# Products with w_o1 and w_o2 in pieces of three matmuls, placed behind the block products; sums of squares for w_g, w_v and w_o2

## The chip, the core and the metric

The kernel runs on one core of a Trainium2 chip. The metric is device time in microseconds (us) of one execution, the median of several.

## What is computed

Softmax attention over channels, then two feed-forward layers on the 6016 tokens. `q` and `k` are normalised over the tokens, a 256x256 softmax is made of them, and `v` is multiplied by it.

```python
def _attn_ref(q, k, v, tau):
    qn = q / (np.linalg.norm(q, axis=1, keepdims=True) + 1e-06)
    kn = k / (np.linalg.norm(k, axis=1, keepdims=True) + 1e-06)
    s = kn.transpose(0, 2, 1) @ qn / tau
    ...
    return (v @ a).astype(np.float32)          # a: softmax of s, 256 x 256

def _moe_ref(x, w_in, w_out):                  # 256 -> 2048 -> 256
    h = x @ w_in
    g = h * (1.0 / (1.0 + np.exp(-1.702 * h)))
    return (g @ w_out).astype(np.float32)

def _moe2_ref(x, w_gate, w_val, w_out):        # 256 -> 1536 -> 256
    gate = 1.0 / (1.0 + np.exp(-(x @ w_gate)))
    val = x @ w_val
    return (gate * val @ w_out).astype(np.float32)
```

In the kernel `w_in` and `w_o1` are the weights of the first layer, `w_g`, `w_v` and `w_o2` those of the second. The weights come as 64-bit floats and are turned into 32-bit floats on the chip.

## The kernel before

Every large product is made of float16 matmuls in threes: both operands are split into a high and a low half, and high by high, high by low and low by high are summed in PSUM (`prod3`). The halves need a common power of two per operand, which is why each weight, each block of `v` and each block of the first layer's output is first reduced to a bound of its size (`w_top`, `w_max`, `v_max`, `y_max`), scaled, and split (a high half by ACT, a low half by DVE).

The tokens are cut into 12 blocks (11 of 512, one of 384). The program has three stretches. First `q` and `k` are read, their product summed over the tokens and the 256x256 softmax made; it is folded into `w_in`, which gives `m_t`. Then the first layer runs block by block. A block has 8 steps; a step makes two rows of 128 hidden channels (`h_unit`), which from block 1 on takes 7 products of 3 matmuls of 256 columns instead of 8 (`seven`, a Strassen-like scheme in which ACT copies a partial sum out of PSUM three times and DVE adds one twice, so that products of one step wait on ACT and DVE; block 0 uses `eight`, plain products of 512 columns). ACT applies the gelu, ACT or DVE rounds to the high half `gh`, DVE makes the low half `gl`. Two steps later `y_unit` multiplies by `w_o1`: 12 matmuls of 512 columns, summed over the block in two PSUM banks, `("acc", 0)` and `("acc", 1)`. Last, the second layer runs the same way: `gv_unit` with 7 products a step and 12 steps a block, and `o_unit`, 6 matmuls of 512 columns with `w_o2` into the same two banks, one step later. During blocks 1 to 6 of the first layer the weights of the second layer are also read, converted (`w_f32`), reduced (`w_top`), scaled and split (`w_split`, `s_piece`), all on DVE and ACT.

The order on every engine is set by a planner (class `Plan`). Operations are written down with what they read and write and with an estimate of their cost. The planner picks the operation that can start first by those estimates; of those on the same engine that could start within `EPS` (0.1 us) of it, it takes the one with the lowest rank. The rank is the place at which the operation was written, plus `plan.delay` at that moment. Each engine then executes its operations strictly in that order on the chip, whatever the real durations are.

Four PSUM banks, `("rot", 0)` to `("rot", 3)`, serve the products of two steps in turn (`ax_pair`); a product of step u+2 waits until ACT has read the pair of step u. Three buffers hold `gh` and `gl` (`NG` = 3), so the high half of step u+3 waits until the product with step u is done; nine further steps of blocks 0 and 1 have buffers of their own. Banks `("acc", 0)` and `("acc", 1)` serve at the start also for the scale of `w_o1` and of the second block of `v` (`p2_ops`, L282 in the trace).

Of the kernel before, what the change touches and what calls it, by code (L numbers as in the profile page):

```python
# [17 lines left out]
PW = 512  # L18
# [8 lines left out]
W_AT, W_STEP = ((1, 4), (2, 4), (3, 2)), 2  # L27
S_AT = (73, 75, 86, 97)
BY_POOL = ("in", "o1")
LOOSE = ("o1",)  # L30

V0_DELAY, V1_DELAY, O1_DELAY, O1_SPLIT, SUM_FIRST = -60, 150, 80, -20, 60


POOL_PEN, GH_DVE = -0.3, 0.3
EPS, HOLD, DMA_WAIT = 0.1, 0.2, 1.2

REBIAS = 2.0**-112
# [123 lines left out]
def fused_kernel(ctx, tc, q, k, vt, tau, w_in, w_o1, w_g, w_v, w_o2, outt):  # L162
# [15 lines left out]
    C, NT = vt.shape  # L178
    CC = C // P
# [31 lines left out]
    T = {}  # L211
# [867 lines left out]
    def pair(u):  # L1079
        f0 = u // 2 * (NB // P) + u % 2  # L1080
        return f0, f0 + 2
# [101 lines left out]
    def y_unit(b, u):  # L1183
        n = blocks[b][1]
        name = f"1_{b}_{u}"
        for z, f in enumerate(pair(u)):
            def mul(e, z=z, f=f):
                for c in range(CC):
                    cs = slice(f * C + c * P, f * C + (c + 1) * P)
                    g = T[name]  # L1190
                    prod3(bank(ACC_BANK[c]), n, wo1_h[:, cs], wo1_l[:, cs], g[0][:, z, :n], g[1][:, z, :n],
                          u == 0 and z == 0, u == NU - 1 and z == 1)

            i = f * C // PW
            r = [g_keys[b, u], ("glo", name), ("wh", "o1", i), ("wl", "o1", i)]
            o = op(mul, ("pe", 0.002532 * n), r=r, w=ACC_BANK)
            if b < 2:
                slot_users.append(o)
        if u == NU - 1:
            def evac(e, c):  # L1200
                nc.scalar.copy(out=y_blk(b)[:, c * n : (c + 1) * n], in_=bank(ACC_BANK[c])[:, :n])

            for c in range(CC):
                op(lambda e, c=c: evac(e, c), ("act", 0.07 + 0.00095 * n), r=[ACC_BANK[c]],
                   w=[("yf", b, c)], after=w_users.get("g", []) + w_users.get("v", []) if b >= YX + 2 else ())
# [49 lines left out]
    for (b, f0), (nm, src) in zip(W_AT, (("o2", w_o2), ("g", w_g), ("v", w_v))):  # L1255
        np_w = src.shape[1] * src.shape[2] // PW
        pos = b * NF1 + f0
        at(*divmod(pos, NF1), w_start(nm, src))
        for i in range(np_w):

            at(*divmod(pos if i < NRAW // 2 else pos + 3 + W_STEP * (i - NRAW // 2), NF1), w_load, nm, i)
            if nm not in LOOSE or not w_src[nm][1]:
                at(*divmod(pos + 2 + W_STEP * i, NF1), w_top, nm, i)
            at(*divmod(pos + 2 + W_STEP * i, NF1), w_f32, nm, i)
        pos += 4 + W_STEP * np_w
        at(*divmod(pos, NF1), w_max, nm)
        pos += 5
        at(*divmod(pos, NF1), lambda nm=nm, after=(): w_scale(nm, after, TOP if nm == "o2" else TOP2))
        if nm == "o2":
            for i in range(np_w):  # L1270
                at(*divmod(pos + 1 + i, NF1), w_split, nm, *[lambda x=x: late_pools()["o2"][x] for x in range(2)], i)
        if nm == "v":
            for x, pos in enumerate(S_AT):
                at(*divmod(pos, NF1), *((s_ratio,) if x == 0 else (s_piece, x - 1)))
# [119 lines left out]
    def o_unit(b, j):  # L1394
        t0, n = blocks[b]
        name = f"2_{b}_{j}"
        keys = ACC_BANK

        def mul(e):
            u = T[name]  # L1400
            for c in range(CC):
                cs = slice(j * C + c * P, j * C + (c + 1) * P)
                prod3(bank(keys[c]), n, *[w[:, cs] for w in late_pools()["o2"]], u[0][:, :n], u[1][:, :n],
                      j == 0, j == NF2 - 1)

        i = j * C // PW
        op(mul, ("pe", 0.002532 * n), r=[g_keys[2, b, j], ("glo", name), ("wh", "o2", i), ("wl", "o2", i)], w=keys)
        if j == NF2 - 1:
            kt = ring("vraw")

            def scale(e):
                T["osc", b] = vec(f"osc{b % 2}")
                nc.vector.tensor_mul(T["osc", b], qb[b], first["ko"])

            def evac(e, c):
                if c == 0:
                    T["ob", b] = v_p.tile([P, CC * NB], F32, tag="v_raw", name=f"ob{b}")
                nc.scalar.activation(
                    out=T["ob", b][:, c * n : (c + 1) * n], in_=bank(keys[c])[:, :n], func=AF.Copy, scale=T["osc", b]
                )  # L1420

            def store(e, c):
                nc.sync.dma_start(out=outt[c * P : (c + 1) * P, t0 : t0 + n], in_=T["ob", b][:, c * n : (c + 1) * n])

            op(scale, ("dve", 0.07), r=[("qb", b), ("k2",)], w=[("osc", b % 2)])
            for c in range(CC):
                kc = kt if c == 0 else ("ob", b, c)
                op(lambda e, c=c: evac(e, c), ("act", 0.07 + 0.00097 * n), r=[keys[c], ("osc", b % 2)] + ([kt] if c else []),
                   w=[kc])
                op(lambda e, c=c: store(e, c), ("dma", 1.0), r=[kc, kt], w=[("out", b, c)])  # L1430
# [60 lines left out]
```

## Time and profile before

| | us |
|---|---|
| median of three runs | 1084.67 |
| lowest and highest | 1082.95, 1086.24 |
| the profiled execution, its own time | 1085.58 |
| its span, first to last instruction | 1083.8 |
| PE busy (7236 matmuls) | 1051.2 |
| DVE busy | 811.4 |
| ACT busy | 724.4 |
| POOL busy | 46.2 |

The profile names an instruction by its line: L1003 are the products of `seven`, L979 to L981 the three matmuls of `prod3` (with `wo` the first layer's second product, with `wo_h` and `wo_l` the second layer's, with `vo,m_t` the plain products of block 0). L1012 are the copies of `seven` on ACT, L1017 its adds on DVE. Matmuls are pipelined: the next one starts before the last has ended, so the distance from start to start is what a matmul costs, and an idle time in brackets counts only from the modelled end of the one before.

### The profile page before, as it was taken

Reading aid. Unit: us, or ns where it says so; the run is one execution under the profiler, and the core shown is the slowest. Engines: PE = TensorE matmul, PEld = TensorE weight load, DVE = VectorE, ACT = ScalarE, POOL = GpSimd, SP = SyncE. Lnnn points to the kernel's source line nnn. Section 1 sums busy time; section 2 is a strip of 40 time slices with the busy share of each in tenths; the row PEclk is TensorE's granted clock in tenths of the full one; section 3 lists DMA queues with packets and bytes.
Section 4 is the critical chain, followed back from the end, with each engine's and each line's share of the span. In section 5 each row is a group of like instructions: output and inputs, shape, how many; then the busy total and the mean of one; then the engine's idle time right before and its main releaser. Section 6 shows DMA issues by size and latency. Waiting matters only on the chain.

```text
span 1083.8 us, 18237 instructions
## 1 busy us (share of the span) xinstructions
PE 1051.2 (97%) x7236; PEld 724.9 (67%) x7236; DVE 811.4 (75%) x1548; ACT 724.4 (67%) x1438; POOL 46.2 (4%) x54
## 2 busy tenths in 40 slices
PE   7988999999999999999999999999999999999998
PEld 6833566666655666666677777777777777777776
DVE  6999999998889677667586666667667667566655
ACT  6786576777757566555576666666767667667665
POOL 1441000000000000000000000000000000000000
PEclk9999999999999999999999999999999999999999
DMA  8940213320000000000000000000000000000000
GB/s 305 371 149 1 98 40 117 98 78 21 1 20 20 1 21 15 1 2 1 1 1 2 21 1 21 20 2 20 1 21 20 1 20 21 1 21 1 21 21 15
DMA packets 16165, 43.63 MB, mean 40 GB/s; under 512 B 1744, under 2 KB 3024, under 8 KB 16080
## 3 DMA queue, kind: packets, MB, share of 16 engines
q1 hardware_dynamic: 16080, 42.47, 11.3%
q8 instruction: 56, 0.92, 0.4%
q14 instruction: 29, 0.24, 0.1%
HBM read 36.31 MB, written 6.16 MB: 39 GB/s over the span
## 4 chain that ended last, share of the span: by engine, by line
PE 81%; DVE 10%; ACT 7%; issue 1%; DMA 1%; SPq 0%; ACTq 0%; DVEq 0%
PE ps L1003 42%; PE ps L980 12%; PE ps L981 11%; PE ps L979 11%; PE ps L717 4%; DVE gl L312 2%; ACT gf L1141 1%; DVE s_t L312 1%; DVE gf L1017 1%; DVE gh L1164 1%; ACT gf L1367 1%; DVE big L499 1%; DMA m_t<-in_q 1%; ACT gh L309 1%; DVE big L611 1%
## 5 line engine op out<-in xcount | busy, mean ns | idle before, releaser
L1003 PE MATMUL ps<-vo,s_t 128*128 128x256 f16 (+1 forms) x3024 | 354.2, 270 | 4.7 <-ACT ps L1012 1.9
L1003 PEld LDWEIGHTS <-s_t 128*128 128x128 f16 x3024 | 292.0, 98 | 73.0 <-issue 9.4
L1017 DVE TENSOR_TENSOR gf<-ps,m_t 128x256 f32<-128x256 f32 (+1 forms) x464 | 192.1, 415 | 151.3 <-PE ps L1003 85.5
L1012 ACT COPY m_t<-ps 128x256 f32<-128x256 f32 (+1 forms) x464 | 167.6, 367 | 149.7 <-PE ps L1003 149.3
L1003 PE MATMUL ps<-vo,m_t 128*128 128x256 f16 (+1 forms) x1848 | 231.7, 271 | 8.2 <-ACT m_t L1012 3.0
L1003 PEld LDWEIGHTS <-m_t 128*128 128x128 f16 x1848 | 179.3, 98 | 69.1 <-issue 12.7
L1385 DVE TENSOR_TENSOR gl<-gf,gh 128x512 f16<-128x512 f32 (+1 forms) x144 | 97.9, 680 | 58.1 <-ACT gh L1380 58.1
L980 PE MATMUL ps<-gl,wo 128*128 128x512 f16 (+1 forms) x348 | 130.2, 374 | 0.5 <-DVE gl L312 0.3
L979 PE MATMUL ps<-gh,wo 128*128 128x512 f16 (+1 forms) x348 | 130.2, 374 | 0.4 <-DVE p_v L285 0.4
L981 PE MATMUL ps<-gh,wo 128*128 128x512 f16 (+1 forms) x348 | 130.2, 374 | 0.0
L1380 ACT CAST gh<-gf 128x512 f16<-128x512 f32 (+1 forms) x135 | 82.3, 610 | 65.2 <-DVE gf L1373 65.0
L312 DVE SCALAR_TENSOR_TENSOR gl<-gf,sgi,gh 128x1024 f16<-128x1024 f32 (+1 forms) x87 | 109.0, 1256 | 3.3 <-ACT gh L309 2.0
L980 PE MATMUL ps<-gl,wo_h 128*128 128x512 f16 (+1 forms) x288 | 107.9, 375 | 0.5 <-DVE gl L1385 0.5
L1367 ACT ACTIVATE gf<-ps,sgb 128x512 f32<-128x512 f32 (+1 forms) x144 | 97.7, 678 | 16.0 <-PE ps L1003 12.5
L979 PE MATMUL ps<-gh,wo_h 128*128 128x512 f16 (+1 forms) x288 | 107.9, 375 | 0.5 <-ACT gh L1380 0.5
L981 PE MATMUL ps<-gh,wo_l 128*128 128x512 f16 (+1 forms) x288 | 107.9, 375 | 0.0
L1373 DVE SCALAR_TENSOR_TENSOR gf<-gf 128x512 f32<-128x512 f32 (+1 forms) x144 | 98.1, 681 | 12.5 <-ACT gf L1367 0.3
L1012 ACT COPY ps<-ps 128x256 f32<-128x256 f32 (+1 forms) x232 | 81.8, 358 | 24.8 <-PE ps L1003 22.4
L1141 ACT ACTIVATE gf<-ps,sgs 128x512 f32<-128x512 f32 (+1 forms) x88 | 59.4, 677 | 36.7 <-PE ps L1003 36.7
L1141 ACT ACTIVATE gf<-gf,sgs 128x512 f32<-128x512 f32 (+1 forms) x88 | 62.3, 711 | 19.2 <-DVE gf L1017 18.3
L981 PEld LDWEIGHTS <-wo 128*128 128x128 f16 x384 | 37.5, 98 | 45.8 <-issue 3.4
L1164 DVE TENSOR_SCALAR gh<-gf,sgi 128x1024 f16<-128x1024 f32 (+1 forms) x61 | 45.2, 743 | 23.2 <-ACT gf L1141 22.7
(217 smaller groups left out, 975.0 us busy)
## 6 DMA issues: line engine op xcount, KB each, us to landing
v_raw<-in_vt SPq DMA_DIRECT2D x11, 512.0 KB, 4.7
out_t<-ob SPq DMA_DIRECT2D x22, 256.0 KB, 2.0
m_t<-in_k SPq DMA_DIRECT2D x10, 512.0 KB, 5.9
m_t<-in_q SPq DMA_DIRECT2D x10, 512.0 KB, 6.8
s_t<-in_w_o SPq DMA_DIRECT2D x6, 512.0 KB, 3.8
s_t<-in_w_g SPq DMA_DIRECT2D x6, 512.0 KB, 3.8
s_t<-in_w_v SPq DMA_DIRECT2D x6, 512.0 KB, 3.9
big<-in_w_in SPq DMA_DIRECT2D x4, 512.0 KB, 6.4
```

The lines of the kernel that those rows point to most:

```text
L312: nc.vector.scalar_tensor_tensor(out=lo, in0=x, scalar=s, in1=h, op0=ALU.mult, op1=ALU.subtract)
L979: nc.tensor.matmul(ps[:, :n], w_h, x_h, start=first, stop=False)
L980: nc.tensor.matmul(ps[:, :n], w_h, x_l, start=False, stop=False)
L981: nc.tensor.matmul(ps[:, :n], w_l, x_h, start=False, stop=last)
L1003: nc.tensor.matmul(dst, l, r, start=start and y == 0, stop=y == 2, skip_group_check=True)
L1012: op(lambda e: nc.scalar.copy(out=dst, in_=bank(key)[:, :w]), ("act", 0.1 + w / 1150), r=[key], w=[wk], after=after)
L1017: nc.vector.tensor_add(val(half), bank(kw)[:, :w], other)
L1141: nc.scalar.activation(out=dst, in_=pair_ap(kx, w) if x == 0 else dst, func=AF.Gelu_apprx_sigmoid, scale=T[sk][0])
L1367: nc.scalar.activation(out=T[kf][:, :n].rearrange("p (x w) -> p x w", x=2), in_=pair_ap(kx, w), func=AF.Sigmoid, scale=T[sk])
L1373: nc.vector.scalar_tensor_tensor(out=v, in0=v, scalar=VSHIFT, in1=T[kf][:, :n], op0=ALU.mult, op1=ALU.mult)
L1380: nc.scalar.copy(out=T[name][0][:, :n], in_=T[kf][:, NB : NB + n])
L1385: nc.vector.tensor_sub(T[name][1][:, :n], T[kf][:, NB : NB + n], T[name][0][:, :n])
```

## The change

`y_unit` and `o_unit` hand each output half (c = 0 or 1) to the planner as an operation of its own, three matmuls that write one bank, where before one operation held both halves and wrote both banks. All of these pieces get 60 added to their rank (`FILL`, `FILL2`), so they stand behind products of `seven` that were written up to 60 operations later. And `w_g`, `w_v` and `w_o2` join `w_o1` in `LOOSE`: the bound on their size is taken from a sum of squares that ACT makes of the converted piece, where before DVE took the largest magnitude of the raw words.

```diff
-LOOSE = ("o1",)
+LOOSE = ("o1", "g", "v", "o2")
...
+FILL, FILL2 = 60, 60
...
     def y_unit(b, u):
...
+        plan.delay = FILL
         for z, f in enumerate(pair(u)):
-            def mul(e, z=z, f=f):
-                for c in range(CC):
+            for c in range(CC):
+                def mul(e, z=z, f=f, c=c):
                     cs = slice(f * C + c * P, f * C + (c + 1) * P)
                     g = T[name]
                     prod3(bank(ACC_BANK[c]), n, wo1_h[:, cs], wo1_l[:, cs], g[0][:, z, :n], g[1][:, z, :n],
                           u == 0 and z == 0, u == NU - 1 and z == 1)
 
-            i = f * C // PW
-            r = [g_keys[b, u], ("glo", name), ("wh", "o1", i), ("wl", "o1", i)]
-            o = op(mul, ("pe", 0.002532 * n), r=r, w=ACC_BANK)
...
+                o = op(mul, ("pe", 0.001266 * n), r=r, w=[ACC_BANK[c]])
...
+        plan.delay = 0
...
-            if nm not in LOOSE or not w_src[nm][1]:
+            if nm not in LOOSE or src.dtype != mybir.dt.int64:
                 at(*divmod(pos + 2 + W_STEP * i, NF1), w_top, nm, i)
...
+        plan.delay = FILL2
+        for c in range(CC):
+            def mul(e, c=c):
+                u = T[name]
                 cs = slice(j * C + c * P, j * C + (c + 1) * P)
                 prod3(bank(keys[c]), n, *[w[:, cs] for w in late_pools()["o2"]], u[0][:, :n], u[1][:, :n],
                       j == 0, j == NF2 - 1)
...
+            op(mul, ("pe", 0.001266 * n), r=[g_keys[2, b, j], ("glo", name), ("wh", "o2", i), ("wl", "o2", i)], w=[keys[c]])
+        plan.delay = 0
```

What the planner makes of it is seen in the order of the instructions. Lines of the changed kernel are one to three higher: its copies are L1013, its adds L1018, its `prod3` L980 to L982, its squares L466.

PE at the end of block 0, after the products of its sixth step (`vo` by `m_t`). Before, the scale of the second block of `v` (`eye_b`) and the products of the seventh step follow:

```order
L981 LDWEIGHTS m_t_85
L981 MATMUL ps_84<-vo_89,m_t_85 128x512
L282 LDWEIGHTS ones_b_249
L282 MATMUL ps_84<-eye_b_91,ones_b_249 128x128
L979 LDWEIGHTS m_t_85
L979 MATMUL ps_84<-vo_89,m_t_85 128x512
```

Now (`gh1_0_0` and `gl1_0_0` are the halves of block 0's first step, `wo1` is `w_o1`):

```order
L982 LDWEIGHTS m_t_85
L982 MATMUL ps_84<-vo_89,m_t_85 128x512
L980 LDWEIGHTS wo1_87
L980 MATMUL ps_84<-gh1_0_0_759,wo1_87 128x512
L981 LDWEIGHTS wo1_87
L981 MATMUL ps_84<-gl1_0_0_760,wo1_87 128x512
L982 LDWEIGHTS wo1_87
L982 MATMUL ps_84<-gh1_0_0_759,wo1_87 128x512
```

A second such piece follows, then the products of the seventh step, then four more pieces, and only then `eye_b`: pieces with c = 0 need only the other bank.

PE in block 3 of the second layer (`wo2` is `w_o2`, `gh2_3_2` the half of step 2). Before, all six matmuls of a step with `w_o2` stand in one run:

```order
L979 LDWEIGHTS wo2_h_882
L979 MATMUL ps_84<-gh2_3_2_7171,wo2_h_882 128x512
L980 LDWEIGHTS wo2_h_882
L980 MATMUL ps_84<-gl2_3_2_7172,wo2_h_882 128x512
L981 LDWEIGHTS wo2_l_883
L981 MATMUL ps_84<-gh2_3_2_7171,wo2_l_883 128x512
L979 LDWEIGHTS wo2_h_882
L979 MATMUL ps_84<-gh2_3_2_7171,wo2_h_882 128x512
L980 LDWEIGHTS wo2_h_882
L980 MATMUL ps_84<-gl2_3_2_7172,wo2_h_882 128x512
```

Now three of them stand between products of `seven` (11 products, 33 matmuls, come before the other three):

```order
L1004 LDWEIGHTS s_t_885
L1004 MATMUL ps_84<-vo_89,s_t_885 128x256
L980 LDWEIGHTS wo2_h_887
L980 MATMUL ps_84<-gh2_3_2_7179,wo2_h_887 128x512
L981 LDWEIGHTS wo2_h_887
L981 MATMUL ps_84<-gl2_3_2_7180,wo2_h_887 128x512
L982 LDWEIGHTS wo2_l_888
L982 MATMUL ps_84<-gh2_3_2_7179,wo2_l_888 128x512
L1004 LDWEIGHTS s_t_885
L1004 MATMUL ps_84<-vo_89,s_t_885 128x256
```

Over the whole program the matmuls of PE form 650 runs of one kind before and 1084 now.

ACT in block 1 of the first layer (L487 and L488 convert a piece of `w_o2`, L1141 and L1142 are gelus). Before:

```order
L1012 COPY ps_84<-ps_84 128x256
L487 ACTIVATE s_t_880<-s_t_880 128x512
L1012 COPY m_t_85<-ps_84 128x256 x2
L1141 ACTIVATE gf1_1_4_1312<-ps_84,sgs1_914 128x512
L1141 ACTIVATE gf1_1_5_1325<-ps_84,sgs1_914 128x512
```

Now:

```order
L1013 COPY m_t_85<-ps_84 128x256 x2
L488 ACTIVATE s_t_885<-s_t_885 128x512
L466 ACTIVATE junk_90,sums_o2_1236<-s_t_885 128x512
L1142 ACTIVATE gf1_1_4_1297<-ps_84,sgs1_970 128x512
L466 ACTIVATE junk_90,sums_o2_1236<-s_t_885 128x512
L1142 ACTIVATE gf1_1_4_1297<-gf1_1_4_1297,sgs1_970 128x512
```

The squares (L466, 18 more of them) stand in ACT's queue among gelus and copies; on DVE the 18 reductions of `w_o2`, `w_g` and `w_v` are gone.

## Rows read from the trace of the kernel before

**Rows 1.** Profile page, part 1: busy us (share of the span) and instructions by engine.

```profile
PE 1051.2 (97%) x7236; PEld 724.9 (67%) x7236; DVE 811.4 (75%) x1548; ACT 724.4 (67%) x1438; POOL 46.2 (4%) x54
```

**Rows 2.** Busy time by stretch: stretch, length, PE, PEld, DVE, ACT, POOL, clock, DMA.

```profile
93.00:105.00 12.00, 9.57 (x38) 3.90 (x36) 11.93 (x18) 8.38 (x10) 0.00 (x0) 0.86 0.01 1
...
145.00:185.00 40.00, 39.34 (x263) 25.52 (x261) 39.11 (x79) 28.19 (x55) 1.05 (x3) 1.00 0.27 93
185.00:225.00 40.00, 38.85 (x253) 24.54 (x252) 39.90 (x81) 30.23 (x56) 2.51 (x3) 1.00 0.34 106
...
303.00:346.00 43.00, 38.79 (x248) 24.83 (x246) 37.32 (x64) 26.96 (x53) 0.68 (x2) 0.96 0.00 1
346.00:555.00 209.00, 208.49 (x1450) 139.27 (x1449) 147.80 (x264) 123.88 (x249) 4.04 (x9) 1.00 0.03 8
```

**Rows 3.** PE in order of time, a dense place: start, duration, line, count.

```profile
401.45 2.46 PE L1003 MATMUL ps<-vo,m_t 128*128 128x256 f16 x21
403.75 0.38 PE L979 MATMUL ps<-gh,wo 128*128 128x512 f16 x1
...
405.04 0.49 PE L1003 MATMUL ps<-vo,m_t 128*128 128x256 f16 x3
```

**Rows 4.** Groups of PE between 119 and 346 us: count, busy, mean ns, idle.

```profile
L1003 PE MATMUL ps<-vo,m_t 128*128 128x256 f16 x924 | 119.7, 275 | 7.6 <-ACT m_t L1012 2.8 <-DVE gf L1017 2.7 <-ACT ps L1012 1.2
L979 PE MATMUL ps<-gh,wo 128*128 128x512 f16 x149 | 56.5, 379 | 0.0
...
L979 PE MATMUL ps<-s_t,wo 128*128 128x512 f16 x24 | 9.1, 379 | 0.0
```

**Rows 5.** Groups of PE between 568 and 1044 us.

```profile
L1003 PE MATMUL ps<-vo,s_t 128*128 128x256 f16 x2722 | 323.5, 272 | 3.3 <-ACT ps L1012 1.9
L979 PE MATMUL ps<-gh,wo_h 128*128 128x512 f16 x262 | 99.3, 379 | 0.0
...
L1003 PE MATMUL ps<-vo,s_t 128*128 128x192 f16 x15 | 1.6, 246 | 0.0
```

**Rows 6.** All engines in order of time, end of block 0.

```profile
89.98 5.01 ACT L309 ACTIVATE wo<-big,s_wo 128x512 f16<-128x512 f32 x8 [0.45 <-DVE s_wo L295]
...
94.90 1.09 ACT L1147 ACTIVATE gf<-ps,sgs 128x1024 f32<-128x1024 f32 x1
...
96.05 0.38 PE L979 MATMUL ps<-vo,m_t 128*128 128x512 f16 x1 [2.07 <-ACT gf L1147]
...
96.47 0.58 PE L981 MATMUL ps<-vo,m_t 128*128 128x512 f16 x1
...
99.84 0.43 PE L980 MATMUL ps<-vo,m_t 128*128 128x512 f16 x1
...
101.49 0.38 PE L979 MATMUL ps<-gh,wo 128*128 128x512 f16 x1 [0.36 <-DVE p_v L285]
```

**Rows 7.** Reductions on DVE (L252): ns min/median/max, first and last start.

```profile
L252 DVE TENSOR_REDUCE sums_o<-s_t x6: 674/676/681, 137.5 to 160.4; 128x1 f32<-128x512 f32 x6
...
L252 DVE TENSOR_REDUCE sums_v<-s_t x6: 676/676/696, 216.6 to 241.5; 128x1 f32<-128x512 f32 x6
```

**Rows 8.** Squares of w_o1 on ACT (L465), in the same columns.

```profile
L465 ACT ACTIVATE junk<-big x8: 612/620/637, 67.1 to 85.2; 128x512 bf16<-128x512 f32 x8
L465 ACT ACTIVATION_READ_ACCUMULATOR junk<-big x8: 185/187/209, 67.6 to 85.7; 128x1 f32 x8
```

**Rows 9.** All engines in order of time, one `s_piece` in block 5.

```profile
308.77 2.29 ACT L309 ACTIVATE s_t<-big,s_wv 128x512 f16<-128x512 f32 x3 [0.80 <-DVE big L617]
...
311.55 2.07 DVE L312 SCALAR_TENSOR_TENSOR s_t<-big,s_wv,s_t 128x512 f16<-128x512 f32 x3
...
314.01 5.43 PE L1003 MATMUL ps<-vo,m_t 128*128 128x256 f16 x33 [2.14 <-DVE gf L1017]
```

**Rows 10.** All engines in order of time, a block's start in the second layer.

```profile
742.29 0.68 ACT L1418 ACTIVATE ob<-ps,osc 128x512 f32<-128x512 f32 x1
...
743.37 0.65 ACT L1012 COPY ps<-ps 128x256 f32<-128x256 f32 x2
...
743.80 0.81 PE L1003 MATMUL ps<-vo,s_t 128*128 128x256 f16 x6 [0.19 <-ACT ps L1012]
```

**Rows 11.** All engines in order of time, the last steps.

```profile
1077.19 0.32 PE L980 MATMUL ps<-gl,wo_h 128*128 128x384 f16 x1 [0.27 <-DVE gl L1385]
...
1078.67 0.32 PE L979 MATMUL ps<-gh,wo_h 128*128 128x384 f16 x1 [0.50 <-ACT gh L1380]
```

More of the change, by code (lines that the diff above doesn't have):

```diff
@@ L1192, in mul @@
                           u == 0 and z == 0, u == NU - 1 and z == 1)
-            i = f * C // PW
-            r = [g_keys[b, u], ("glo", name), ("wh", "o1", i), ("wl", "o1", i)]
-            o = op(mul, ("pe", 0.002532 * n), r=r, w=ACC_BANK)
-            if b < 2:
-                slot_users.append(o)
+                i = f * C // PW
+                r = [g_keys[b, u], ("glo", name), ("wh", "o1", i), ("wl", "o1", i)]
+                o = op(mul, ("pe", 0.001266 * n), r=r, w=[ACC_BANK[c]])
+                if b < 2:
+                    slot_users.append(o)
+        plan.delay = 0
         if u == NU - 1:
@@ L1397, in o_unit @@
         keys = ACC_BANK
-        def mul(e):
-            u = T[name]
-            for c in range(CC):
+        i = j * C // PW
+        plan.delay = FILL2
+        for c in range(CC):
+            def mul(e, c=c):
+                u = T[name]
                 cs = slice(j * C + c * P, j * C + (c + 1) * P)
@@ L1404, in mul @@
                       j == 0, j == NF2 - 1)
-        i = j * C // PW
-        op(mul, ("pe", 0.002532 * n), r=[g_keys[2, b, j], ("glo", name), ("wh", "o2", i), ("wl", "o2", i)], w=keys)
+            op(mul, ("pe", 0.001266 * n), r=[g_keys[2, b, j], ("glo", name), ("wh", "o2", i), ("wl", "o2", i)], w=[keys[c]])
+        plan.delay = 0
         if j == NF2 - 1:
```

## The prediction

> **What bounds the kernel now.** I read the page's first part, then busy time by stretch, then PE in order of time, and only then the waits. PE is busy for 97% of the span [rows 1], but a matmul's row lasts longer than its turn, so I took the distance from start to start. In a dense place 21 matmuls of 256 columns take 2.30 us, 0.109 us each, six of 512 columns 1.29 us, 0.215 us each, and the step from one kind to the other adds nothing [rows 3]. With these two prices the matmuls of a stretch can be summed and set against its length. From 119 to 346 us: 924 x 0.109 = 100.7, and 518 of 512 columns (three lines of 148 or 149 and three of 24 or 25) x 0.215 = 111.4, together 212.1 of 227 us: **14.9 us without a matmul** [rows 4]. From 568 to 1044 us: 2722 x 0.109, 786 (three lines of 262) x 0.215 and 15 of 192 columns at three quarters of 0.109 make 466.9 of 476 us: **9.1 us** [rows 5]. From 346 to 555 PE is busy 208.49 of 209.00: nothing [rows 2]. So PE bounds the kernel nearly everywhere, and what can be won is its holes: some 15, 9, and a few at the two places below.
>
> What makes the holes differs. Between 145 and 225 us DVE is busy 79.0 of 80 us [rows 2]: there it is as much the bound as PE, since the second layer's weights pass through it. Later DVE and ACT are loaded by about two thirds and a hole comes only where a burst of other work stands in their queue ahead of a copy or add: the S pieces [rows 9], the start of each block in the second layer [rows 10].
>
> The Trainium skill judges this otherwise: Perfetto Trace Analysis, section Identifying the Most-Contended Engine, takes the share of weight loads for the better measure of PE's headroom. That share is 139.27 of 209 us between 346 and 555 [rows 2] and would leave a third of the stretch; the starts there are back to back, so I keep to the rows.
>
> **A, end of block 0.** The products of the seventh step wait 2.07 us for the gelu at 94.90, which stands behind eight splits of `w_o1` on ACT (5.01 us); then the clock is 1.2 GHz for a while (granted 0.86 in this stretch) and eight distances from 96.47 to 99.84 take 3.37 us instead of 8 x 0.215 = 1.72 [rows 2, 6]. Now two pieces, 6 x 0.215 = 1.29 us, stand in the hole; their weights were split from 90 us on. The wait that is left, some 0.8 us, is far shorter than the two after which this trace shows a slow clock (2.07 here, 2.14 in rows 9), so I take the clock to stay: 1.29 + 1.65. The later wait of 0.36 for the bank of `eye_b` [rows 6] goes too, since c = 0 pieces no longer need that bank. Sum 3.3 us; at least 1.3 if the clock falls all the same, at most 4.1.
>
> **B, blocks 1 to 6 (119 to 346 us).** The 18 reductions of 0.676 us leave DVE: 12.2 us [rows 7]. ACT gets 18 squares of 0.620 with 0.187 for reading the sum: 14.5 us [rows 8], onto an engine that is busy 58 of 80 us where DVE is full [rows 2]. The planner prices a square at 0.61, so ACT lags its plan by 0.2 us at each; and each waits in ACT's queue for a DVE shift of its piece, with gelus and copies behind it. The squares of `w_o1` run at that plain price in a stretch where DVE is nearly as full [rows 8]. Price of the squares to PE: from 0 to 18 x 0.81 = 14.5; I take 1, because PE now has pieces in stock whenever a product waits.
>
> The holes: with DVE no longer the bound and up to three steps of pieces in stock (three buffers), half of those before 303 us should go. The largest single place is the S piece: three splits on ACT (2.29), then splits on DVE (2.07 of them in one row), and PE stands 2.14 us and then runs at 1.2 GHz (granted 0.96 over 43 us, so 1.7 us lost) [rows 2, 9]. The change doesn't touch this burst. In the new order products of the same steps again stand behind it, now with seven pieces ahead of the one that waits; adding up DVE's queue by these durations I expect a hole of 1 to 1.5 us, too short for the clock. So 14.9 becomes about 6, plus the 1 for squares: gain 8, bounds 0 and 14.9.
>
> ScalarE: Activation LUTs in the Trainium skill, section Rules for kernel authors, speaks against this part: simple arithmetic and maxima belong on VectorE. The rows agree on the price of one (0.807 against 0.676 us), and by that rule alone the move would cost 18 x 0.131 = 2.4 us of engine time, making the gain 5 or 6 here; but the engine that is full is DVE.
>
> **C, blocks 7 to 11 (346 to 555 us).** No hole to fill, so only something to lose. From the order I took, for each copy, the PE work between the product it reads and the product that needs it. Copies with less than 1 us of it: 45 before, 89 now in this stretch. Those before lost next to nothing (208.49 of 209.00 busy), but in 119 to 346 us about 50 such copies go with half of the holes, some 0.1 us each. So 0 to 44 x 0.1 = 4.4 us lost; I take 1, near the rows of this same stretch.
>
> **D, second layer (568 to 1044 us).** The holes come where ACT's two evacuations `ob` and a rounding stand ahead of copies [rows 10]; the two waits at such a start are 0.3 us each from start to start, and there are ten blocks of them. The copies with less than 1 us of PE work behind them fall from 258 to 98 in the new order, most now having 1.3 us, since a piece stands in between. Scaled by that, 9.1 becomes 9.1 x 98/258 = 3.5: gain 5.6, bounds 0 and 9.1.
>
> **E, the end.** Before, the last two steps with `w_o2` wait for their halves, 0.27, 0.50 and once more 0.27 us idle, 1.5 us from start to start [rows 11]. Now nine pieces stand after the last product; seven of them, 7 x 3 matmuls of 384 columns at three quarters of 0.215, 3.4 us, run while the halves of the last step are made. Gain 1.5, at least 0.5.
>
> Reading and storing move by a piece at most and are not waited for. The matmuls are the same in number.
>
> **Sum.** 3.3 + 8 - 1 + 5.6 + 1.5 = 17.4 us off the profiled execution of 1085.58: 1068.2. That execution is 0.9 above the median of 1084.67, so I predict **1067 us**.
>
> **Rivals.**
>
> 1. All holes go: 4.1 + 14.9 + 9.1 + 1.5 = 29.6, so 1055. For it: stock is always there and the planner knows the waits. Against it: DVE's S bursts are longer than the stock at some places.
>
> 2. The holes move. The bursts on ACT and DVE stay as they are, products now stand as early as the planner's estimates allow, and those are too short for the squares at least (0.61 against 0.81). Then C costs its 4.4, D gives half, B half: 3.3 + 4 - 4.4 + 2.8 + 1.5 = 7, so about 1077. Against it: the 45 close copies between 346 and 555 ran nearly without a wait.
>
> 3. Slower: the squares hold up ACT. If each of the 18 waits for a full DVE queue (one reduction's length, 0.68) and PE waits for that and for the square, 18 x 1.49 = 26.8 us are lost against 18.4 won elsewhere: 1093. It decides from 1.0 us per square on. For it: a strict queue with copies behind, DVE full. Against it: the squares of `w_o1` ran beside an equally full DVE, and PE's stock.
>
> 4. No effect: pieces stand where they stood. The order shows that they don't (1084 runs instead of 650); only if all gains were covered by losses would it be 1084.
>
> **How the numbers follow.** Forecast, 1061 to 1073: 0.60. Rival 1, 1053 to 1061: 0.13. Rival 2, 1073 to 1081: 0.16. Rival 4: 0.04. Rival 3: 0.07. A measurement tells 0.3%, 3.3 us, from no change: faster 0.89, same 0.04, slower 0.07. The range leaves out rivals 3 and 4 and the outer half of rivals 1 and 2's tails: 1057 to 1077.
>
> **What would show it.** A: no idle row of 2 us near 96 and a granted clock of 1.00 there. B: DVE below 95% between 145 and 225 us, L466 with 18 more rows, no hole of 2 us at the S pieces, clock 1.00 after 300 us. C: PE's busy share between 346 and 555 unchanged. D: no copies named as PE's releaser at block starts. E: no wait in the last nine pieces. It would be wrong if PE's waits name ACT in blocks 1 to 3 for over 5 us in all (rival 3), or if the number of short waits on copies grows (rival 2).

## The result, and the profile after

| | us |
|---|---|
| before, median, measured beside it | 1085.45 |
| after, median (1058.84 to 1060.1) | 1059.43 |
| ratio after to before, 95% interval | 0.9764 (0.9745 to 0.9783) |
| profiled execution after, its own time | 1059.32 |
| its span | 1057.5 |

The changed kernel is 26 us faster. The forecast was 1067 with a range of 1057 to 1077: the sign and the range hold, but the sum gave 17.4 us and the profiled spans differ by 26.3. The time lies in the band that I had given to rival 1 (all holes go, 1053 to 1061).

The page's first part of the changed kernel, as in [rows 1]: busy us, share, instructions.

```profile
PE 1036.3 (98%) x7236; PEld 722.8 (68%) x7236; DVE 805.5 (76%) x1535; ACT 710.4 (67%) x1469; POOL 49.8 (5%) x54
```

The matmuls are the same in number. Busy time by stretch after (stretch, length, PE, PEld, DVE, ACT, POOL, clock, DMA), to be set beside [rows 2]:

```profile
93.00:105.00 12.00, 11.15 (x53) 5.00 (x52) 11.93 (x17) 7.82 (x9) 0.00 (x0) 1.00 0.00 1
145.00:185.00 40.00, 40.00 (x271) 26.28 (x270) 38.02 (x77) 33.34 (x71) 2.01 (x3) 1.00 0.32 105
185.00:225.00 40.00, 38.75 (x259) 25.19 (x258) 38.02 (x77) 30.66 (x66) 2.00 (x3) 1.00 0.30 91
303.00:346.00 43.00, 42.97 (x295) 28.58 (x293) 37.32 (x65) 30.97 (x61) 1.64 (x2) 1.00 0.05 13
346.00:555.00 209.00, 208.30 (x1474) 141.30 (x1472) 147.50 (x277) 128.64 (x257) 6.08 (x9) 1.00 0.02 6
545.00:1020.00 475.00, 474.95 (x3584) 349.69 (x3582) 327.96 (x618) 307.38 (x691) 0.64 (x1) 1.00 0.03 12
```

The clock stays at 1.00 in the two places where it had been 0.86 and 0.96 (e10 below shows that this is not the change's doing alone), and the second layer has lost its holes: the matmuls that start in the last stretch come to 473.2 of 475 us by their prices.

**Where the 26 us come from.** The programs run the same matmuls in nearly the same sequence, so the time can be split by place. I give each float16 matmul its price (0.215 us for 512 columns, 0.109 for 256, three quarters of these for 384 and 192), add them up from the first product of block 0 on, and compare when two kernels have the same sum behind them. A positive number is time won against the kernel before in that part of the work; the parts are named by their times before. Before the first product 0.6 us were won, the tail after the last matmul is the same. "e" kernels are the experiments below.

| us won in | 68–119, end of block 0 | 119–133, start of block 1 | 133–346, blocks 1–6 | 346–555, blocks 7–11 | 555–1070, second layer | 1070–1080, end |
|---|---|---|---|---|---|---|
| predicted | 3.3 | in the next | 8 | −1 | 5.6 | 1.5 |
| changed kernel | 3.4 | −2.1 | 11.7 | 1.3 | 9.6 | 1.7 |
| e1 order, no squares | 3.4 | −2.1 | 9.3 | 1.5 | 10.1 | 1.7 |
| e2 squares alone | −1.5 | 0.0 | 2.3 | 0.0 | 0.1 | 0.0 |
| e3 pieces, rank 0 | 0.1 | −0.2 | 5.8 | 1.7 | −4.1 | 0.1 |
| e4 sixes, rank 60 | 0.0 | 0.0 | 12.5 | 0.7 | 7.8 | −0.1 |
| e5 first layer's rank alone | 3.5 | −2.1 | 11.6 | 1.3 | −3.1 | 0.1 |
| e7 rank 30 | 3.7 | −2.6 | 11.5 | 1.2 | 8.7 | 1.5 |
| e8 rank 120 | 3.4 | −1.6 | 13.3 | −1.7 | 6.5 | 1.7 |
| e9 split of v early | 3.6 | −0.4 | 13.8 | 1.5 | 10.1 | 1.7 |
| e13 the same, no squares | 3.5 | −0.4 | 7.0 | 1.1 | 9.9 | 1.7 |
| e10 before, ob twice | 0.1 | 0.0 | 1.0 | 0.0 | −10.0 | 0.0 |
| e11 after, ob twice | 3.6 | −2.1 | 12.2 | 1.3 | 2.6 | 1.7 |
| e14 the same, told | 3.6 | −2.1 | 11.6 | 1.3 | 7.7 | 0.9 |

The table also says how well it can be read: blocks 1 to 6 are the same program in the changed kernel, e5, e11 and (but for buffers) e14, and give 11.7, 11.6, 12.2, 11.6; e10 is there the kernel before and gives 1.0, all of it at the S piece and from the clock (see e10). I read nothing from less than about 1 us.

**End of block 0**, all engines in order of time, answering to [rows 6]. Two pieces with `wo` stand ahead of the products that wait for the gelu; the last matmul of them starts at 94.26:

```profile
94.26 0.38 PE L982 MATMUL ps<-gh,wo 128*128 128x512 f16 x1
...
94.34 1.09 ACT L1148 ACTIVATE gf<-ps,sgs 128x1024 f32<-128x1024 f32 x1
...
95.48 0.38 PE L980 MATMUL ps<-vo,m_t 128*128 128x512 f16 x1 [0.85 <-ACT gf L1148]
...
95.70 0.38 PE L981 MATMUL ps<-vo,m_t 128*128 128x512 f16 x1
```

The wait is 0.85 us instead of 2.07, and the next start follows after 0.22 us: the clock is at 2.4 GHz.

**Start of block 1.** Here time is lost that the prediction did not see:

```profile
119.93 0.38 PE L982 MATMUL ps<-s_t,wo 128*128 128x512 f16 x1
120.14 0.27 PE L1004 MATMUL ps<-vo,m_t 128*128 128x256 f16 x1
120.34 1.01 DVE L313 SCALAR_TENSOR_TENSOR vo<-v_raw,s_v,vo 128x768 f16<-128x768 f32 x1
...
121.41 0.70 PE L1004 MATMUL ps<-vo,m_t 128*128 128x256 f16 x5 [0.99 <-DVE vo L313]
...
122.32 3.44 PE L1004 MATMUL ps<-vo,m_t 128*128 128x256 f16 x30 [0.21 <-ACT ps L1013]
```

PE has used up block 0's pieces by 120 us. DVE's split of the second block of `v` stands later in its queue and begins at 120.34 us, where it began at 115.51 before, while PE is 3.4 us earlier; and the block's first 75 matmuls run without a piece between them.

**One S piece** in block 5, answering to [rows 9]:

```profile
300.31 2.07 DVE L313 SCALAR_TENSOR_TENSOR s_t<-big,s_wv,s_t 128x512 f16<-128x512 f32 x3
...
300.49 1.15 PE L1004 MATMUL ps<-vo,m_t 128*128 128x256 f16 x9
301.47 0.38 PE L980 MATMUL ps<-gh,wo 128*128 128x512 f16 x1
...
302.30 0.75 DVE L1018 TENSOR_TENSOR gf<-ps,m_t 128x256 f32<-128x256 f32 x2
...
302.77 0.82 PE L1004 MATMUL ps<-vo,m_t 128*128 128x256 f16 x6
```

The same three splits hold DVE for 2.07 us and the adds wait behind them; PE fills the time with nine matmuls of `seven` (three products) and two pieces, without a bracket.

**A block's start in the second layer**, answering to [rows 10]:

```profile
729.55 0.69 ACT L1423 ACTIVATE ob<-ps,osc 128x512 f32<-128x512 f32 x1 [0.43 <-PE ps L982]
...
730.13 0.36 ACT L1013 COPY m_t<-ps 128x256 f32<-128x256 f32 x1
...
730.33 0.38 PE L980 MATMUL ps<-gh,wo_h 128*128 128x512 f16 x1
```

The copy still stands behind the evacuation; a piece now runs on PE while the copy is made. **At the end** the last nine pieces show no bracket. The squares, count and ns min/median/max, answering to [rows 8]; `w_o1`'s eight and those of `w_g` and `w_v` share a row:

```profile
L466 ACT ACTIVATE junk<-big x20: 612/628/640, 66.5 to 233.7; 128x512 bf16<-128x512 f32 x20
...
L466 ACT ACTIVATE junk<-s_t x6: 614/620/627, 140.6 to 157.5; 128x512 bf16<-128x512 f32 x6
```

### The profile page after: what moved, and what is told of

Read it like the earlier page. It is cut to its first block, busy times and chain, and to the rows that moved or that the text cites. A ratio compares the mean times of both kernels' runs of the same rounds, so it can differ in the third digit from the quotient of the medians.

```text
span 1057.5 us, 18643 instructions
## 1 busy us (share of the span) xinstructions
PE 1036.3 (98%) x7236; PEld 722.8 (68%) x7236; DVE 805.5 (76%) x1535; ACT 710.4 (67%) x1469; POOL 49.8 (5%) x54
## 3 DMA queue, kind: packets, MB, share of 16 engines
q1 hardware_dynamic: 16080, 42.47, 11.5%
## 4 chain that ended last, share of the span: by engine, by line
PE 87%; DVE 7%; ACT 3%; DMA 1%; issue 1%; SPq 0%; ACTq 0%; DVEq 0%
PE ps L1004 47%; PE ps L982 12%; PE ps L980 12%; PE ps L981 12%; PE ps L718 3%; DVE s_t L313 1%; DMA m_t<-in_q 1%; DVE gl L313 1%; DVE ms L956 1%; DMA s_t<-in_w_v 1%; DVE big L500 0%; DVE mf L951 0%; ACT wo L310 0%; ACT junk L466 0%; DVE sums_in L253 0%
## 5 line engine op out<-in xcount | busy, mean ns | idle before, releaser
L1004 PE MATMUL ps<-vo,s_t 128*128 128x256 f16 (+1 forms) x3024 | 371.0, 270 | 0.6 <-ACT m_t L1013 0.6
L1018 DVE TENSOR_TENSOR gf<-ps,m_t 128x256 f32<-128x256 f32 (+1 forms) x464 | 191.6, 415 | 142.2 <-PE ps L1004 102.8
L1004 PE MATMUL ps<-vo,m_t 128*128 128x256 f16 (+1 forms) x1848 | 239.8, 270 | 2.1 <-DVE vo L313 1.0
L1013 ACT COPY m_t<-ps 128x256 f32<-128x256 f32 (+1 forms) x464 | 168.5, 365 | 93.7 <-PE ps L1004 92.4
L980 PE MATMUL ps<-gh,wo 128*128 128x512 f16 (+1 forms) x348 | 130.2, 374 | 1.3 <-ACT y_f L1204 1.3
L982 PE MATMUL ps<-gh,wo 128*128 128x512 f16 (+1 forms) x348 | 130.2, 374 | 0.0
L980 PE MATMUL ps<-gh,wo_h 128*128 128x512 f16 (+1 forms) x288 | 107.9, 375 | 0.0
L982 PE MATMUL ps<-gh,wo_l 128*128 128x512 f16 (+1 forms) x288 | 107.9, 375 | 0.0
L1013 ACT COPY ps<-ps 128x256 f32<-128x256 f32 (+1 forms) x232 | 84.8, 367 | 16.1 <-PE ps L1004 14.5
L1142 ACT ACTIVATE gf<-gf,sgs 128x512 f32<-128x512 f32 (+1 forms) x88 | 61.9, 710 | 15.7 <-DVE gf L1018 14.8
L1165 DVE TENSOR_SCALAR gh<-gf,sgi 128x1024 f16<-128x1024 f32 (+1 forms) x64 | 47.6, 744 | 26.3 <-PE ps L982 22.5
L982 PEld LDWEIGHTS <-wo 128*128 128x128 f16 x384 | 37.6, 98 | 43.6
L1142 ACT ACTIVATE gf<-ps,sgs 128x512 f32<-128x512 f32 (+1 forms) x88 | 59.3, 674 | 11.7 <-PE ps L1004 11.2
```

Of the source, the lines that this page charges most:

```text
L980: nc.tensor.matmul(ps[:, :n], w_h, x_h, start=first, stop=False)
L982: nc.tensor.matmul(ps[:, :n], w_l, x_h, start=False, stop=last)
L1004: nc.tensor.matmul(dst, l, r, start=start and y == 0, stop=y == 2, skip_group_check=True)
L1013: op(lambda e: nc.scalar.copy(out=dst, in_=bank(key)[:, :w]), ("act", 0.1 + w / 1150), r=[key], w=[wk], after=after)
L1018: nc.vector.tensor_add(val(half), bank(kw)[:, :w], other)
L1142: nc.scalar.activation(out=dst, in_=pair_ap(kx, w) if x == 0 else dst, func=AF.Gelu_apprx_sigmoid, scale=T[sk][0])
```

## The experiments

**e1, the order alone.**

```diff
-LOOSE = ("o1", "g", "v", "o2")
+LOOSE = ("o1",)
```

> The changed kernel with its pieces and ranks, but w_g, w_v and w_o2 bounded by reductions on DVE again, as before. By the same count of matmuls the changed kernel gained 3.4 us at the end of block 0, lost 2.1 at the start of block 1, gained 11.8 in the rest of blocks 1 to 6, 1.2 in blocks 7 to 11, 9.1 in the second layer and 1.6 at the end. Theory (order): the stock of pieces fills PE's waits, and DVE matters only where it is full (145 to 225 us before); without the squares the first place, the second layer and the end stay as they are and blocks 1 to 6 keep more than half of the 11.8: 1060 to 1066 us, DVE above 97% between 145 and 225 us. Rival (relief of DVE): the holes of blocks 1 to 6 come from a full DVE, so without the squares nearly all of the 11.8 is lost: 1069 to 1072. Rival (squares cost): they hold up copies on ACT, so without them it is faster than 1058.

Measured: 1061.84 us (1061.11 to 1062.22), 0.978 (0.9767 to 0.9794) of before. All but 2.4 us of the gain is the order's, and what is lost is lost in blocks 1 to 6. DVE is full there (two stretches, columns as above):

```profile
185.00:225.00 40.00, 39.02 (x257) 24.88 (x256) 39.85 (x80) 25.94 (x53) 2.08 (x3) 1.00 0.30 94
225.00:265.00 40.00, 38.28 (x255) 24.66 (x254) 39.09 (x86) 27.24 (x52) 2.10 (x3) 1.00 0.13 40
```

**e2, the squares alone.** The kernel before with

```diff
-LOOSE = ("o1",)
+LOOSE = ("o1", "g", "v", "o2")
...
-            if nm not in LOOSE or not w_src[nm][1]:
+            if nm not in LOOSE or src.dtype != mybir.dt.int64:
```

> The kernel before with the squares alone: products with w_o1 and w_o2 in sixes at their old places, sums of squares on ACT for w_g, w_v and w_o2. Theory (order): PE has no stock, each square stands before copies that PE waits for, and what DVE gives back is worth little: 1080 to 1088 us, the hole of 2 us at the end of block 0 unchanged. Rival (relief of DVE): 1073 to 1077, the holes between 145 and 346 us halved. Rival 3 of the prediction without stock to cover it: 18 x 1.49 = 27 us lost, 1105 to 1112.

Measured: 1083.86 us, 0.9982 (0.9973 to 0.9992). Blocks 1 to 6 win 2.3 us against the trace of the kernel before, about what the squares win on top of the order (2.4, e1 against the changed kernel). Against e10, which is there the kernel before with the clock kept up at the S piece, it is 1.3. The end of block 0 loses 1.5: PE's waits there (in all, times, longest) name the bank of `eye_b` with 2.0 us where [rows 6] has 0.36.

```profile
PE ps L979 <- ACT gf L1147: 2.1, 1, 2.1
PE ps L979 <- DVE p_v L285: 2.0, 1, 2.0
```

That is the clock and not the squares. After the first wait the starts stay 0.22 us apart, so PE is 1.7 us earlier at the bank, which comes free when DVE has read `p_v`, and waits that much longer. The slow clock comes only after this second wait, and there nothing hides it (order of time):

```profile
100.59 0.38 PE L979 MATMUL ps<-gh,wo 128*128 128x512 f16 x1 [2.05 <-DVE p_v L285]
...
102.14 0.63 PE L979 MATMUL ps<-gh,wo 128*128 128x512 f16 x1
102.57 0.63 PE L980 MATMUL ps<-gl,wo 128*128 128x512 f16 x1
```

**e3, pieces without the rank.**

```diff
-FILL, FILL2 = 60, 60
+FILL, FILL2 = 0, 0
```

> The changed kernel with FILL and FILL2 at 0: pieces of three and squares, but the pieces keep the rank of the place where they are written. The order still alternates (1124 runs of one kind, 1084 in the changed kernel), but a piece goes in as soon as it can. Theory (stock): what fills the holes is that pieces are held back until a product waits; without it half or more of the gain in blocks 1 to 6 and in the second layer goes: 1068 to 1076 us. Rival (alternation): what counts is that a piece of 0.65 us stands behind each copied product; then it is within 4 us of the changed kernel: 1056 to 1063.

Measured: 1082.81 us, 0.9976 (0.9967 to 0.9985). Worse than either expectation: PE's runs alternate more often than in the changed kernel, and the second layer is 4.1 us slower than before. PE's waits in it:

```profile
PE ps L1004 <- ACT m_t L1013: 4.0, 10, 0.4
PE ps L1004 <- ACT gf L1370: 3.9, 9, 0.6
```

Ten blocks, one wait of each kind in nearly all. Alternation by itself is worth next to nothing in sum (1 us against e2), but not at each place: against e2 it wins 3.5 us in blocks 1 to 6 and 1.7 in blocks 7 to 11, and loses 4.2 in the second layer. At the end of block 0 the hole is filled and the clock kept, as in the changed kernel, and 3.2 us are won up to the place that is 108 us before; two waits for the halves of a piece (1.28 and 1.15 us, at 108.87 and 110.40 us) take them back.

**e4, the rank without pieces.** Six matmuls in one operation that writes both banks, as before, with

```diff
+        plan.delay = FILL
...
+        plan.delay = FILL2
```

> The changed kernel with the six matmuls of a step joined in one operation again, held back by the same 60 ranks; squares as changed. Theory (stock): holding back is enough at most places, and only finer spreading is lost: 1062 to 1070 us. Rival (alternation): with sixes there are 630 runs of one kind instead of 1084, half as many copies are covered, and the second layer and blocks 1 to 6 lose most of their gain: 1072 to 1080.

Measured: 1064.99 us (1063.52 to 1066.74), 0.9811 (0.9797 to 0.9824), as the theory has it. What the pieces add is not finer spreading in general: blocks 1 to 6 do as well without. They are worth 3.4 us at the end of block 0, of which 2.1 are given back, 1.8 in the second layer and 1.8 at the end. In block 0 no six stands ahead of the seventh step (it writes both banks, and `eye_b` has one of them); the hole stays, and in this trace the slow clock too (order of time):

```profile
94.90 0.38 PE L980 MATMUL ps<-vo,m_t 128*128 128x512 f16 x1 [2.08 <-ACT gf L1148]
...
96.17 0.63 PE L981 MATMUL ps<-vo,m_t 128*128 128x512 f16 x1
...
96.59 0.63 PE L982 MATMUL ps<-vo,m_t 128*128 128x512 f16 x1
```

**e8 and e7, more and less rank.** `FILL, FILL2 = 120, 120` and `30, 30`. They set two measures against each other: the prediction's count of products close behind their copy (here with DVE's adds and the gates counted too, hence 299 and 118 where the prediction has 258 and 98), and how long the halves of a step lie ready in the second layer, from the end of `gl` on DVE to the first matmul that reads the step's halves.

> The changed kernel with FILL and FILL2 at 120 in place of 60: pieces stand behind products written up to 120 operations later. Counted in the planner's order over the second layer, as in the prediction's part C, the products with less than 1 us of PE work behind the one their copy reads are 328 here, 118 in the changed kernel, 299 in the kernel before. Theory (stock: what counts is how long the halves of a piece lie ready; their median lead in the second layer is 1.1 us before, 6.6 in the changed kernel): the lead grows or stays and the second layer keeps its 9 us of gain: 1056 to 1062 us. Rival (close copies, the prediction's own measure): the second layer has as many as before and its gain is gone: 1067 to 1071, with copies on ACT named in PE's waits there.

> The changed kernel with FILL and FILL2 at 30. Close products in the second layer: 93, fewer than the changed kernel's 118. Theory (stock): half the rank gives a shorter lead, some 3 to 4 us, and part of the gain goes in both layers: 1060 to 1066 us. Rival (close copies): as good or better than the changed kernel, 1056 to 1060.

Measured: 1063.62 us, 0.9798 (0.9785 to 0.9812), above the theory's range and below the rival's, and 1061.49 us, 0.9782 (0.9767 to 0.9796), in the theory's range. All kernels side by side:

| second layer | close products | halves ready, median (10th percentile) us | us won |
|---|---|---|---|
| before | 299 | 1.1 (0.1) | 0 |
| e3 rank 0 | 265 | 1.1 (0.1) | −4.1 |
| e7 rank 30 | 93 | 5.0 (3.5) | 8.7 |
| changed, rank 60 | 118 | 6.6 (4.2) | 9.6 |
| e8 rank 120 | 328 | 6.4 (2.0) | 6.5 |
| e4 sixes, rank 60 | 316 | 4.4 (2.4) | 7.8 |

Where many products are close, 6.5 and 7.8 us are won all the same if halves lie ready, and 4.1 lost if they don't. The count of close products is the wrong measure. But against rank 60, rank 120 loses 3 us in blocks 7 to 11 and 3 in the second layer, which neither theory had; why is open.

**e5, the first layer alone.**

```diff
-FILL, FILL2 = 60, 60
+FILL, FILL2 = 60, 0
```

> The changed kernel with FILL2 at 0: pieces of w_o2 keep their written rank, those of w_o1 are held back by 60. With both at 0 the second layer lost 4.0 us against the kernel before by the same count of matmuls, where the changed kernel gained 9.65. Theory (the gains of the layers are independent; the stock decides): 1059.4 + 13.7 = 1073, range 1070 to 1075. Rival (the second layer gains since the first hands it a better start): 1060 to 1066.

Measured: 1073.44 us (1073.12 to 1074.54), 0.9891 (0.9877 to 0.9904): the layers' gains are independent.

**e10 and e11, a burst on ACT doubled**, in the kernel before and in the changed one; the evacuation of each bank is done twice:

```diff
             def evac(e, c):
...
-                nc.scalar.activation(
+                for _ in range(2):
+                    nc.scalar.activation(
```

> The kernel before with each evacuation of the second layer's banks into ob done twice on ACT: 22 more of 0.684 us and two of 0.58, one pair at each block's end, unknown to the planner, so the order stays. It measures what a burst on ACT costs PE. Some 1.1 us of it lie on the tail after the last matmul. Theory (stock: halves lie ready for 1.1 us in the median here, so a burst reaches PE): most of 11 x 1.37 = 15 us is lost: 1094 to 1102 us. Rival (PE feels only the copies with a product close behind them, and of these only the first after a burst): 0.3 us a block, 1088 to 1091.

> The changed kernel with the same evacuations done twice. The halves of a piece lie ready for 6.6 us in the median here and for 4.2 at the tenth percentile. Theory (stock): the pieces cover the burst of 1.37 us at nearly every block, and only the tail grows: 1060 to 1063 us. Rival (holding back only moved the products early enough by the planner's estimates, so a burst it doesn't know reaches PE as before): as much lost as in the kernel before with the same edit, 1067 to 1075.

Measured: 1095.87 us (before: 1085.59), and 1066.89 us, against 1059.43 without. The burst costs PE 10.0 us in the kernel before and 7.0 in the changed one, 9.6 less 2.6. The theory that ready halves cover a burst falls: they lay ready for 6.6 us in e11 too. PE's waits in the second layer, first e10's, then e11's, whose ten come to some 5.4 us when counted from start to start:

```profile
PE ps L1003 <- ACT ps L1012: 10.7, 10, 1.2
```

```profile
PE ps L1004 <- ACT m_t L1013: 3.8, 10, 0.4
```

PE runs its queue in order, and a product whose copy is late stops it. At one of e11's block starts (order of time):

```profile
730.51 1.43 ACT L1424 ACTIVATE ob<-ps,osc 128x512 f32<-128x512 f32 x2
730.68 1.14 PE L1004 MATMUL ps<-vo,s_t 128*128 128x256 f16 x9 [0.38 <-ACT m_t L1013]
...
731.66 0.38 PE L980 MATMUL ps<-gh,wo_h 128*128 128x512 f16 x1
```

The halves of the piece that starts at 731.66 had been ready since 724.84, and PE stood still all the same: the piece is next in its queue only after these nine matmuls.

e10 shows one thing more, since up to the second layer it is the kernel before. Its long waits in the first layer are those of the kernel before, yet the granted clock stays at 1.00 (order of time at the end of block 0, then the two stretches of [rows 2] that had 0.86 and 0.96):

```profile
96.27 0.38 PE L979 MATMUL ps<-vo,m_t 128*128 128x512 f16 x1 [2.08 <-ACT gf L1147]
...
101.71 0.38 PE L979 MATMUL ps<-gh,wo 128*128 128x512 f16 x1 [2.05 <-DVE p_v L285]
```

```profile
93.00:105.00 12.00, 7.87 (x38) 3.45 (x36) 11.93 (x18) 8.60 (x10) 0.00 (x0) 1.00 0.01 1
303.00:346.00 43.00, 38.29 (x253) 24.42 (x251) 38.19 (x68) 27.84 (x55) 0.67 (x2) 1.00 0.00 1
```

At the end of block 0 that gains nothing (0.1 us in the table): from the seventh step to the start after the bank of `eye_b` it takes 5.44 us with the slow clock (96.05 to 101.49, [rows 6]) and 5.44 without it. DVE sets that start, and what the slow clock costs there is taken off the wait. At the S piece the kept clock is worth 1.0 us.

**e14, the same burst, told to the planner.**

```diff
-("act", 0.07 + 0.00097 * n), r=[keys[c], ("osc", b % 2)]
+("act", 0.14 + 0.00194 * n), r=[keys[c], ("osc", b % 2)]
```

> The changed kernel with the second layer's evacuations done twice, as in the run before (1066.9 us, of it 7.0 us lost in the second layer, 0.54 us at one wait per block), but with their price told to the planner: 0.14 + 0.00194 n in place of 0.07 + 0.00097 n. The theory that ready halves cover a burst by themselves has fallen. Amended theory (PE executes in a fixed order, so a piece covers a wait only where the planner foresaw it and put the piece in front): with the price told, most of the 7.0 us come back: 1060 to 1063 us, no wait of over 0.2 us at the blocks' starts. Rival (the burst is longer than what the pieces can cover, whatever the planner knows): 1065 to 1068.

Measured: 1063.66 us (1062.25 to 1064.26), 0.9793 (0.9779 to 0.9806). The time is just above the theory's range, but the place decides: 5.1 of the 7.0 us are back, and between 560 and 1030 us no wait of PE shows any more. So a stock of pieces is worth what the planner's estimates of the bursts are worth: it puts a piece where it foresees a wait. Where the last 1.9 us went was not followed.

**e9, the second block of `v` split earlier.**

```diff
-V0_DELAY, V1_DELAY, O1_DELAY, O1_SPLIT, SUM_FIRST = -60, 150, 80, -20, 60
+V0_DELAY, V1_DELAY, O1_DELAY, O1_SPLIT, SUM_FIRST = -60, 60, 80, -20, 60
```

> The changed kernel with V1_DELAY at 60 in place of 150: the split of the second block of v stands 30 instructions earlier on DVE. By the same count of matmuls the changed kernel gives 2.1 of the 3.4 us won at the end of block 0 back at the start of block 1, where PE waits 1.0 us for DVE's split of vo and some 0.3 us four times more. Theory (that start waits for the split alone): up to 2 us are won, 1057 to 1058.5. Rival (DVE is full from 93 to 145 us, so what is put ahead makes the halves of block 0 or the sums of m_t late instead): no gain or a loss, 1059 to 1063.

Measured: **1054.8 us** (1053.91 to 1055.66), 0.9717 (0.9703 to 0.973), the best kernel of the study and better than the theory had it. 1.7 of the 2.1 us at the start of block 1 return, and blocks 1 to 6 win 2.1 more. The split now begins at 101.32 us, and products of block 1 start at 110.55, while pieces of block 0 are left; two stretches:

```profile
105.00:145.00 40.00, 39.64 (x252) 24.44 (x251) 38.64 (x71) 30.46 (x55) 0.79 (x2) 1.00 0.21 64
...
185.00:225.00 40.00, 40.00 (x269) 26.14 (x268) 39.61 (x79) 30.49 (x67) 1.48 (x3) 1.00 0.30 91
```

PE is busy for all 40 us of the second, where the changed kernel had 38.75.

**e13, e9 with the reductions on DVE.** `LOOSE = ("o1",)` in e9.

> The changed kernel with V1_DELAY at 60 (1054.8 us) and with w_g, w_v and w_o2 bounded by reductions on DVE, as before. PE had no hole of over 0.3 us between 128 and 539 us with the squares. Theory (the relief of DVE is worth in blocks 1 to 6 what it was worth at the two places tried: 2.4 us with the pieces held back, 2.35 without): 1056 to 1058.5. Rival (with the split of v early the stock covers DVE too): 1054 to 1055.5. Rival (DVE, full from 145 to 225 us, becomes the bound once PE has no other hole): over 1060.

Measured: 1062.19 us, 0.9788 (0.9774 to 0.9803): 7.4 us slower than e9, 6.8 of them in blocks 1 to 6, as the last rival has it:

```profile
145.00:185.00 40.00, 40.00 (x270) 26.25 (x269) 39.51 (x82) 26.23 (x52) 1.91 (x3) 1.00 0.28 93
185.00:225.00 40.00, 37.73 (x241) 23.29 (x239) 38.96 (x76) 27.50 (x53) 1.42 (x3) 1.00 0.32 100
```

DVE is busy 78.5 of 80 us and PE loses 2.3. Set beside e1 this points to DVE as the bound: in the work up to 185 us (times before) e13 is 1.8 us ahead of e1, up to 225 and 265 us the two agree within 0.2. With the reductions on DVE the earlier split of `v` is worth nothing (1062.19 against 1061.84 us); without them it is worth 4.6.

## Why the prediction was right, and where its sum was wrong

**What bounds the kernel** held: PE's starts, and what can be won is its holes. The prices hold too: between 545 and 1020 us the matmuls that start make 473.2 of 475 us by them, though the kind changes some 500 times; the start of a piece follows the last matmul of 256 columns by 0.109 us in the mean, and the start after a piece follows its last matmul by 0.216, so a change of kind costs nothing. The Trainium skill (Perfetto Trace Analysis, Identifying the Most-Contended Engine) names the weight loads' share as one of two measures of headroom, beside the share of the peak arithmetic rate. That share is 349.69 of these 475 us, and the starts leave 1.8 us: the rows decide against it.

**A, end of block 0:** predicted 3.3, measured 3.4. The first term holds: the wait is 0.85 us where I put 0.8. The other two, 1.65 for the kept clock and 0.36 for the bank of `eye_b`, are one: with the clock kept the kernel before waits 2.05 us for the bank (e10), so the slow clock cost it nothing, and what is won is that pieces stand where PE waited for the bank. The sum came out because 1.65 + 0.36 is that same wait; that the clock was a price of its own was wrong. What the step left out is the next one: the split of `v` stands 4.8 us later in DVE's queue, PE comes 3.4 earlier, and 2.1 us went back. e9 shows that the place of the split was the cause: 1.7 of the 2.1 return.

**B, blocks 1 to 6:** predicted 8, measured 11.7 − 2.1 = 9.6. Mis-sized was the share of holes that would go. I let half go and kept a hole of 1 to 1.5 us at the S piece; there is none, since the adds' burst is covered by three products and two pieces. The slow clock there, 1.7 us in the prediction, was worth 1.0, and not every execution has it: e10 has the same wait without it. The squares were not a price of 1 us: net of DVE's relief they won some 1.3 us alone (e2 against e10) and 2.4 on top of the order (e1). DVE's share between 145 and 225 us, forecast below 95%, is 76.04 of 80, just at it: PE starts 530 matmuls there instead of 516. By the Trainium skill's rule (ScalarE: Activation LUTs, Rules for kernel authors), which puts simple arithmetic and maxima on VectorE, the squares would have cost time, 18 x 0.131 = 2.4 us of engine time by the durations of one: 0.62 + 0.187 us on ACT against 0.676 on DVE. Those durations agree with the rule, but the kernel's time went the other way, because DVE was the full engine (e13).

**C, blocks 7 to 11:** predicted −1, measured +1.3. Two steps failed. 89 close copies at 0.1 us each cost nothing that can be read here. And there were holes: I read busy time, 208.49 of 209.00, where the starts by their prices make only 206.6 us before, some 2 us less than the stretch. Pieces alone win 1.7 of it (e3).

**D, second layer:** predicted 5.6, measured 9.6, the largest miss. The step that failed is 9.1 × 98/258, holes in proportion to close copies. e3, e4 and e8 show that this count does not set the holes. What does is whether the planner has a piece at hand where it foresees a wait: held back, the halves lie ready for 6.6 us instead of 1.1, and the piece is put in front of the product (e14: foreseen, 5.1 of 7.0 us return; e11: not foreseen, they are lost). The loss at rank 120 is not explained by it. That it was the rank and not the pieces is shown by e3 against e4.

**E, the end:** predicted 1.5, measured 1.7; in e3 and e4 it is 0.1 and −0.1, so it needs pieces and rank together.

**The sum** missed in one direction: 1.6 us in B (net of the 2.1), 2.3 in C, 4.0 in D. The time lies 2.4 us above the lower end of the range, and 2.1 us of that is the loss at the start of block 1, which the prediction did not see; with the split moved (e9) it is 1054.8, outside. That the range held was in part luck.

**The rivals.** Rival 1 was nearest: "the planner knows the waits" was its ground, and the experiments bear that out; I gave it 0.13 since DVE's bursts seemed longer than the stock. Rival 2 (close copies) fell with its measure. Rival 3 fell: PE's waits between 105 and 540 us name ACT for 1.9 us in all, 1.3 of them for an evacuation (`y_f`). Rival 4 was excluded by the order, and e3 shows that a very different order may still come out within 3 us of the old time.

Open stay the loss at rank 120, 1.9 us in e14, and the 0.6 us before the first product, which the change does not touch and which varies from −0.5 to +1.2 us over the kernels here.

## What to carry to other kernels

Where an engine executes in a fixed order and waits for others in many short places, look for work on it that nobody needs soon, and hold it back in the order, so that whoever sets the order has it at hand; cutting it small without that won 5.2 us in the first layer here and lost 4.2 in the second (e3 against e2). Such filler covers the waits that the order's estimates foresee, so bursts must be priced truly. And follow a gain to the next place that another engine sets: here 2.1 of 3.4 us went back there until the split of `v` was moved too.

## What the runs showed of the hardware

PE's granted clock after a wait of about 2 us is not the same from one trace to the next. After 2.07 us (before), 2.08 us (e4) and 2.05 us (e2, the second wait) seven or eight starts of 512 columns in a row lie 0.42 to 0.43 us apart, which is 1.2 GHz; after 2.14 us (before, the S piece) the granted clock also falls. After 2.08 us (e2, the first wait) and 2.08, 2.05 and 2.15 us (e10) they stay at 0.22, or 0.11 for 256 columns, which is 2.4 GHz, with a granted clock of 1.00. e10 is up to there the kernel before, so the order of the work does not decide it, and what does is not shown. After the wait of 0.85 us in the changed kernel, and after the other waits of up to 1.76 us between block 0 and the end in all the kernels here, the clock stays at 2.4 GHz. The prediction's argument, that the wait left is shorter than those with a slow clock behind them, fits these rows.

In these traces a slow stretch was paid for only where no other engine set PE's next start: at the end of block 0 it cost the kernel before nothing, since the next start waits for DVE anyway, 5.44 us behind either way; at the S piece it cost 1.0 us; in e2, with no such wait behind it, 1.5.
